# A new program order for a transformer kernel: another choice of scheduler settings per piece

## The chip, the cores and the metric

The kernel runs on one core of a Trainium2 chip. The core has five engines that run their own instruction streams and meet only at semaphores: TensorE (PE) multiplies matrices, VectorE (DVE) and ScalarE (ACT) work element by element, GpSimd (POOL) does so more slowly, and SyncE (SP) starts the transfers between HBM and the on-chip memory. Matmuls write into eight banks of 128x512 numbers of 32 bits (the tensor ps), which VectorE and ScalarE read. The metric is the device time of one execution in microseconds, lower is better.

## What is computed

Two transformer layers on the same weights: x has 2048 rows of 512 numbers, attention has 32 heads of 16, the hidden layer has 1792.

```
for _ in range(2):
    n = layernorm(x);  q, k, v = split(n @ wqkv)
    p = softmax(q @ k.T / 4)              # per head, 2048 x 2048
    x = x + (p @ v) @ wo
    x = x + gelu(layernorm(x) @ w1 + b1) @ w2 + b2
```

Almost all of the element work is the exponential of the scores: 2 layers, 32 heads, 2048 x 2048 numbers each.

## The kernel before

**Cells.** The transposed scores are made in cells of 128 keys by 512 queries (a cell of the last stage joins two heads of 256 queries). There are 4096 of them, each one matmul (score, L1404; the instruction appears at L1413). A pass has up to 64 cells: four heads, each in one group of 32 rows of TensorE's array, by 16 blocks of keys. Cells of different row groups run beside each other; two or three of them make a slot, in as many banks that lie side by side.

**Two ways through the exponential.** ScalarE's exp (exps, instruction at L1853) takes the two or three banks of a slot in one instruction and writes pt. VectorE's way takes one cell at a time: dfirst (L1568, instruction at L1570) turns the score into the bits of a 16-bit power of two in the buffer du; then, for a pair of such cells, dchain (L1673) makes three shifted copies. The first copy is made by GpSimd (L1687) or VectorE, the other two by VectorE in one instruction (L1692), or one each by GpSimd (L1700) and VectorE (L1698). The four copies are multiplied on TensorE by values with four weights (v and vc), so that a VectorE cell needs four value matmuls where a ScalarE cell needs one (pvs, L1869, instructions at L1917; L1925 pads a round of four with zero columns). Where TensorE would stand idle for long, fill matmuls (L1401) keep it running. Some buffers lie over tensors that are not in use at the time, so the same work shows up as du, kt, v, q or g.

**Which cells may go to VectorE.** Blocks of keys 4 to 8 in layer 0 and 1, 4, 7, 10, 13 in layer 1 (KD), so 5 of 16; any of them may also go to ScalarE.

**The rest.** Layer norms (L760 to L786), projections and the hidden layer (matmuls at L653, read out by VectorE), gelu on ScalarE (L1128, with a table load before and after), output projection and residuals run between the cells, as the due times in post allow (a share of the scores of the stage, when). Weights stream through four buffers (wload, on SyncE).

**What sets the order.** No engine chooses at run time. At build time a list scheduler (_Sched.run, L450) plays the whole kernel through with a cost for each instruction (0.065 + 0.4267n us for an exp of n banks, 0.682 for dfirst, 0.15 + 0.45n for a GpSimd shift of n cells, 0.2132 for a round of matmuls), always issues what can start first, by priority among what can start now, and so writes one fixed program per engine, with the waits that the data need. It decides as it goes which cells VectorE takes: attach adds cells to a score group that is about to be issued, as long as banks and buffers are free; swap exchanges the last cell of a group of three for a VectorE cell; solo issues one alone. It also decides which engine makes the shifts.

**Settings.** 29 numbers steer these decisions, named in NAMES. Some examples: SWAP, DMAX, BOTH, SOLO, BACK, SIDE, ALONE, TOL, BACKLOG, OPENING, TAIL and AHEAD say when VectorE may take a cell; PSHIFT, PMORE and DUMORE when GpSimd makes shifts; ROUNDS, PVP, PTURG, DUURG, DULOW, DWIDE, RWIDE and PTLOW when value products run and how many rounds in one go; FPRIO, MID and EVAC rank projections; SLACK, LATE and QUEUE concern the scores' own urgency and the banks. A row of ROWS is one setting of all 29. The scores are cut into 160 pieces of 25.6 cells, and PIECES names the row for each. turn (L1446) loads the next row when take (L1450) has counted enough scores. Row 0 is the plain setting; most others differ from it in one to four numbers.

Of the kernel before, what the change touches and what calls it, by code (L numbers as in the profile page):

```python
# [63 lines left out]
    (0.2, 0.3, 0.7, 0.2, 9, 18, 10, 2, 6, 1, 1, 2, 2, 5, 1.5, 1.4, 0.4, 2, 3.5, 24, 3, 4, 0.4, 1.0, 0, 1, 2, 1, 2,),  # L64
    (0.35, 0.3, 0.7, 0.2, 9, 18, 10, 2, 6, 1, 1, 2, 2, 5, 1.5, 1.4, 0.4, 2, 3.5, 24, 3, 4, 0.4, 1.0, 0, 1, 2, 1, 2,),
    (0.5, 0.2, 0.7, 0.2, 9, 18, 10, 2, 6, 1, 1, 2, 2, 5, 1.5, 1.4, 0.4, 2, 3.5, 24, 3, 4, 0.4, 1.0, 0, 1, 2, 1, 2,),
    (0.5, 0.4, 0.7, 0.2, 9, 18, 10, 2, 6, 1, 1, 2, 2, 5, 1.5, 1.4, 0.4, 2, 3.5, 24, 3, 4, 0.4, 1.0, 0, 1, 2, 1, 2,),
    (0.5, 0.3, 0.7, 0.05, 9, 18, 10, 2, 6, 1, 1, 2, 2, 5, 1.5, 1.4, 0.4, 2, 3.5, 24, 3, 4, 0.4, 1.0, 0, 1, 2, 1, 2,),
    (0.5, 0.3, 0.7, 0.2, 9, 10, 10, 2, 6, 1, 1, 2, 2, 5, 1.5, 1.4, 0.4, 2, 3.5, 24, 3, 4, 0.4, 1.0, 0, 1, 2, 1, 2,),
    (0.5, 0.3, 0.7, 0.2, 9, 14, 10, 2, 6, 1, 1, 2, 2, 5, 1.5, 1.4, 0.4, 2, 3.5, 24, 3, 4, 0.4, 1.0, 0, 1, 2, 1, 2,),  # L70
    (0.5, 0.3, 0.7, 0.2, 9, 18, 6, 2, 6, 1, 1, 2, 2, 5, 1.5, 1.4, 0.4, 2, 3.5, 24, 3, 4, 0.4, 1.0, 0, 1, 2, 1, 2,),
    (0.5, 0.3, 0.7, 0.2, 9, 18, 8, 2, 6, 1, 1, 2, 2, 5, 1.5, 1.4, 0.4, 2, 3.5, 24, 3, 4, 0.4, 1.0, 0, 1, 2, 1, 2,),
    (0.5, 0.3, 0.7, 0.2, 9, 18, 10, 1.2, 6, 1, 1, 2, 2, 5, 1.5, 1.4, 0.4, 2, 3.5, 24, 3, 4, 0.4, 1.0, 0, 1, 2, 1, 2,),
    (0.5, 0.3, 0.7, 0.2, 9, 18, 10, 2, 3, 1, 1, 2, 2, 5, 1.5, 1.4, 0.4, 2, 3.5, 24, 3, 4, 0.4, 1.0, 0, 1, 2, 1, 2,),
    (0.5, 0.3, 0.7, 0.2, 9, 18, 10, 2, 6, 2, 1, 2, 2, 5, 1.5, 1.4, 0.4, 2, 3.5, 24, 3, 4, 0.4, 1.0, 0, 1, 2, 1, 2,),
    (0.5, 0.3, 0.7, 0.2, 9, 18, 10, 2, 6, 3, 1, 2, 2, 5, 1.5, 1.4, 0.4, 2, 3.5, 24, 3, 4, 0.4, 1.0, 0, 1, 2, 1, 2,),
    (0.5, 0.3, 0.7, 0.2, 9, 18, 10, 2, 6, 1, 1, 2, 2, 3, 1.5, 1.4, 0.4, 2, 3.5, 24, 3, 4, 0.4, 1.0, 0, 1, 2, 1, 2,),
# [4 lines left out]
    (0.5, 0.3, 0.7, 0.2, 9, 18, 10, 2, 6, 1, 1, 2, 2, 5, 1.5, 1.4, 0.4, 2, 2.0, 24, 3, 4, 0.4, 1.0, 0, 1, 2, 1, 2,),  # L82
    (0.5, 0.3, 0.7, 0.2, 9, 18, 10, 2, 6, 1, 1, 2, 2, 5, 1.5, 1.4, 0.4, 2, 3.5, 12, 3, 4, 0.4, 1.0, 0, 1, 2, 1, 2,),
    (0.5, 0.3, 0.7, 0.2, 9, 18, 10, 2, 6, 1, 1, 2, 2, 5, 1.5, 1.4, 0.4, 2, 3.5, 24, 3, 4, 0.0, 1.0, 0, 1, 2, 1, 2,),
    (0.5, 0.3, 0.7, 0.2, 9, 18, 10, 2, 6, 1, 1, 2, 2, 5, 1.5, 1.4, 0.4, 2, 3.5, 24, 3, 4, 0.4, 1.5, 0, 1, 2, 1, 2,),
# [4 lines left out]
    (0.5, 0.3, 0.7, 0.2, 9, 18, 10, 2, 6, 1, 1, 2, 2, 5, 1.5, 1.4, 0.4, 2, 3.5, 24, 3, 4, 0.4, 1.0, 0, 1, 2, 1, 1,),  # L90
    (0.5, 0.3, 0.7, 0.2, 9, 18, 10, 2, 6, 1, 1, 2, 2, 5, 1.5, 1.4, 0.4, 2, 3.5, 24, 3, 4, 0.4, 1.0, 0, 1, 2, 1, 5,),
    (0.5, 0.4, 0.7, 0.2, 9, 18, 10, 2, 6, 1, 1, 2, 2, 8, 1.5, 1.4, 0.4, 2, 3.5, 24, 3, 4, 0.4, 1.0, 9, 1, 2, 2, 2,),
    (0.5, 0.3, 0.7, 0.5, 9, 18, 10, 2, 6, 1, 1, 2, 2, 5, 1.5, 1.4, 0.4, 2, 3.5, 24, 3, 4, 0.4, 1.0, 9, 1, 2, 1, 2,),
    (0.5, 0.3, 0.7, 0.05, 9, 18, 10, 2, 6, 3, 1, 2, 2, 5, 1.5, 1.4, 0.4, 2, 3.5, 24, 3, 4, 0.4, 1.0, 0, 1, 2, 1, 2,),
    (0.5, 0.3, 0.7, 0.35, 9, 18, 10, 2, 6, 1, 1, 2, 2, 5, 1.5, 1.7, 0.4, 3, 3.5, 24, 3, 4, 0.4, 1.0, 0, 1, 2, 1, 2,),
    (0.5, 0.3, 0.7, 0.2, 9, 18, 10, 2, 6, 1, 1, 2, 2, 5, 1.5, 1.7, 0.4, 3, 3.5, 24, 3, 4, 0.4, 1.0, 0, 1, 2, 1, 2,),
    (0.5, 0.3, 0.7, 0.2, 9, 18, 10, 2, 6, 1, 1, 2, 2, 5, 1.5, 1.4, 0.4, 2, 3.5, 24, 3, 4, 0.4, 1.0, 0, 2, 2, 1, 1,),
    (0.5, 0.3, 0.7, 0.2, 9, 18, 10, 2, 6, 1, 0, 2, 2, 5, 1.5, 1.4, 0.4, 2, 3.5, 24, 3, 4, 0.4, 0.6, 0, 1, 2, 1, 2,),
    (0.5, 0.3, 0.7, 0.2, 9, 18, 10, 1.2, 6, 1, 1, 2, 2, 5, 1.5, 1.4, 0.4, 2, 3.5, 24, 3, 4, 0.4, 1.0, 0, 2, 2, 1, 2,),
    (0.5, 0.3, 0.8, 0.2, 9, 18, 10, 2, 6, 1, 0, 2, 2, 5, 1.5, 1.4, 0.4, 2, 3.5, 24, 3, 4, 0.4, 1.0, 0, 1, 2, 1, 2,),  # L100
    (0.5, 0.3, 0.7, 0.2, 9, 18, 10, 2, 6, 3, 1, 2, 2, 5, 1.5, 1.4, 0.4, 1, 3.5, 24, 3, 4, 0.0, 1.0, 0, 1, 2, 1, 2,),
    (0.5, 0.3, 0.7, 0.2, 9, 10, 10, 2, 6, 0, 1, 2, 2, 5, 1.5, 1.4, 0.4, 2, 3.5, 24, 3, 4, 0.4, 1.0, 0, 1, 2, 1, 2,),
    (0.5, 0.3, 0.7, 0.2, 9, 18, 10, 2, 6, 1, 1, 2, 2, 5, 2.2, 0.9, 0.4, 2, 3.5, 24, 3, 6, 0.4, 1.0, 0, 1, 2, 1, 2,),
    (0.5, 0.3, 0.55, 0.2, 9, 18, 10, 2, 6, 1, 1, 2, 3, 5, 1.5, 1.4, 0.4, 2, 3.5, 24, 3, 4, 0.4, 1.0, 0, 1, 2, 1, 2,),
    (0.5, 0.3, 0.7, 0.2, 9, 18, 13, 2, 6, 1, 1, 2, 2, 5, 1.5, 0.9, 0.4, 2, 3.5, 24, 3, 4, 0.4, 1.0, 0, 1, 2, 1, 2,),
    (0.5, 0.3, 0.7, 0.2, 9, 18, 10, 2, 6, 1, 1, 2, 2, 8, 1.5, 1.4, 0.4, 1, 3.5, 24, 3, 4, 0.4, 1.0, 0, 1, 2, 1, 2,),
    (0.5, 0.2, 0.7, 0.2, 9, 10, 10, 2, 6, 1, 1, 2, 2, 5, 0.9, 1.4, 9.5, 2, 3.5, 24, 3, 4, 0.4, 1.0, 0, 1, 2, 1, 2,),
    (0.5, 0.3, 0.7, 0.2, 9, 18, 10, 2, 6, 1, 1, 3, 2, 5, 1.5, 1.4, 0.4, 2, 3.5, 24, 3, 4, 0.4, 0.6, 0, 1, 2, 2, 2,),
    (0.5, 0.2, 0.7, 0.2, 9, 18, 10, 2, 6, 1, 1, 2, 2, 5, 1.5, 1.4, 0.4, 2, 3.5, 24, 3, 4, 0.4, 1.0, 1.0, 1, 2, 1, 2,),
    (0.5, 0.3, 0.7, 0.05, 9, 18, 10, 2, 3, 1, 1, 2, 2, 5, 1.5, 1.4, 9.5, 2, 3.5, 24, 3, 4, 0.4, 1.0, 0, 1, 2, 1, 2,),  # L110
    (0.5, 0.3, 0.7, 0.2, 9, 18, 10, 2, 6, 1, 1, 2, 2, 8, 1.5, 1.4, 0.4, 2, 6, 24, 3, 6, 0.4, 1.0, 0, 1, 2, 0.5, 2,),
    (0.5, 0.3, 0.7, 0.2, 9, 18, 10, 2, 6, 1, 1, 2, 2, 5, 1.5, 1.4, 0.4, 1, 3.5, 24, 3, 4, 0.0, 1.0, 0, 1, 2, 1, 2,),
    (0.35, 0.3, 0.8, 0.2, 9, 18, 10, 2, 6, 1, 1, 2, 2, 5, 1.5, 1.4, 0.4, 2, 3.5, 24, 5, 4, 0.4, 1.0, 0, 1, 0, 1, 2,),
    (0.5, 0.3, 0.7, 0.2, 9, 18, 10, 2, 6, 1, 1, 2, 2, 5, 1.5, 1.4, 0.4, 1, 3.5, 32, 3, 4, 0.4, 1.0, 9, 1, 2, 1, 1,),
# [6 lines left out]
    (0.5, 0.3, 0.7, 0.5, 9, 18, 10, 2, 6, 2, 1, 2, 2, 5, 1.5, 1.4, 0.4, 2, 3.5, 24, 3, 4, 0.4, 1.0, 0, 1, 2, 1, 2,),  # L121
    (0.5, 0.3, 0.7, 0.2, 9, 18, 10, 2, 6, 2, 1, 2, 3, 5, 1.5, 1.4, 0.4, 2, 3.5, 24, 3, 4, 0.4, 1.0, 0, 1, 2, 1, 2,),
    (0.5, 0.3, 0.7, 0.35, 9, 18, 10, 2, 6, 1, 1, 2, 2, 5, 1.5, 0.9, 0.4, 3, 3.5, 24, 3, 4, 0.4, 1.0, 0, 1, 2, 1, 3,),
)
PIECES = (10, 10, 15, 18, 18, 43, 56, 38, 30, 38, 38, 28, 8, 0, 60, 60, 48, 21, 43, 35, 46, 0, 1, 45, 45, 49, 4, 11, 41, 25, 57, 24, 20, 31, 15, 1,
          35, 2, 2, 27, 44, 0, 2, 2, 29, 12, 17, 0, 0, 1, 1, 0, 4, 59, 43, 0, 26, 34, 37, 57, 41, 34, 13, 46, 47, 47, 47, 0, 34, 49, 13, 19, 17, 32,
          36, 41, 27, 17, 23, 52, 0, 11, 0, 0, 44, 52, 12, 54, 40, 25, 37, 0, 0, 39, 0, 50, 50, 26, 0, 0, 33, 50, 6, 18, 22, 0, 0, 25, 25, 0, 0, 5,
          42, 16, 53, 0, 36, 12, 0, 55, 34, 18, 53, 3, 0, 46, 0, 0, 58, 0, 0, 0, 46, 25, 25, 41, 44, 13, 12, 12, 17, 20, 12, 12, 7, 54, 25, 28, 0, 0,
          58, 29, 10, 10, 8, 51, 0, 9, 14, 0)
# [513 lines left out]
class _Plan:  # L643
# [802 lines left out]
    def turn(self):  # L1446
        self.piece += 1
        globals().update(zip(NAMES, ROWS[PIECES[self.piece]]))

    def take(self, c):  # L1450
        self.scored += 1
        self.left[c[0]] -= 1
        self.due[c[0]] += 1
        if self.piece + 1 < len(PIECES) and self.scored * len(PIECES) >= (self.piece + 1) * self.total:
            self.turn()
# [573 lines left out]
```

## Time and profile before

| | us |
|---|---|
| median of 3 runs | 1489.41 (1488.92 to 1489.61) |
| the profiled execution | 1490.43 |
| its span, first to last instruction | 1488.6 |
| ScalarE busy | 1457.6 |
| TensorE busy | 1432.6 |
| VectorE busy | 1353.7 |
| GpSimd busy | 942.6 |

Shares are of the span. The busy time of TensorE is to be read with care: its matmuls overlap and their ends are modelled. A group's line in the profile shows the line of code, engine, operation, what is written and read, the count, the busy time, the mean time of one instruction, and the idle time of the engine before it with what ended it.

### The profile page before, as it was taken

To read this page: it belongs to the slowest core of one execution; us is meant where nothing else is said; L and a number is where in the kernel's file an instruction comes from. 1 tells how busy PE (TensorE), PEld (TensorE's weight loads), DVE (VectorE), ACT (ScalarE), POOL (GpSimd) and SP (SyncE) were. 2 spreads that over 40 slices of the span, in tenths; PEclk is the share of its full clock that TensorE was granted. 3 is DMA by queue.
4 is the path that set the end of the run, shared out by engine and by line. 5 is a ranking of instruction groups with operands and counts; after the bars stand their busy time and mean duration, and the time that the engine had idled before them with its cause. 6 is when DMAs were issued, how large, how long until landed. Compare 5 with 4: busy or idle time off the path is not lost.

```text
span 1488.6 us, 46274 instructions
## 1 busy us (share of the span) xinstructions
PE 1432.6 (96%) x20012; PEld 436.7 (29%) x20012; DVE 1353.7 (91%) x2332; ACT 1457.6 (98%) x1387; POOL 942.6 (63%) x1032
## 2 busy tenths in 40 slices
PE   8999999999999999999999999999999999999999
PEld 2222222222222222222222222222222222334345
DVE  6589999999998999989879899999989999999994
ACT  7999999999999999999999999999999999999996
POOL 4347657676665776757556575667667667766751
PEclk9999999999999999999999999999999999999999
DMA  6100001153121430214421431001143104411021
GB/s 171 30 2 2 1 15 31 40 157 91 37 44 58 143 87 27 55 38 132 117 65 44 144 107 37 23 2 37 37 129 100 51 23 129 143 25 44 17 66 38
DMA packets 135798, 94.47 MB, mean 63 GB/s; under 512 B 36525, under 2 KB 134574, under 8 KB 135598
## 3 DMA queue, kind: packets, MB, share of 16 engines
q1 hardware_dynamic: 135598, 91.52, 22.1%
q8 instruction: 160, 2.62, 0.7%
q14 instruction: 40, 0.33, 0.1%
HBM read 79.70 MB, written 4.19 MB: 56 GB/s over the span
## 4 chain that ended last, share of the span: by engine, by line
ACT 49%; PE 37%; DVE 12%; POOL 1%; DMA 1%; issue 1%; SPq 0%
ACT pt L1853 42%; PE ps L653 12%; PE ps L1413 12%; PE ps L1917 12%; DVE du L1570 5%; ACT g L1128 3%; DVE du L1692 2%; DVE kt L1570 1%; ACT kt L1853 1%; ACT q L1853 1%; ACT L1128 1%; PE ps L1401 1%; DVE x L1167 1%; ACT L1853 1%; DVE g L1107 0%
## 5 line engine op out<-in xcount | busy, mean ns | idle before, releaser
L1853 ACT ACTIVATE pt<-ps 128x1024 bf16<-128x1024 f32 (+1 forms) x1253 | 1306.9, 1177 | 8.0 <-PE ps L1413 6.1
L1570 DVE TENSOR_SCALAR du<-ps 128x512 uint16<-128x512 f32 x853 | 564.9, 680 | 40.3 <-PE ps L1413 35.8
L1687 POOL TENSOR_SCALAR du<-du 128x1024 uint16<-128x1024 uint16 (+1 forms) x429 | 445.8, 1044 | 232.4 <-DVE du L1570 97.4
L1413 PE MATMUL ps<-qp,kt 32*128 32x512 bf16 x4096 | 548.4, 384 | 25.2 <-ACT pt L1853 13.6
L1917 PE MATMUL ps<-pt,v 128*17 128x512 bf16 (+1 forms) x3159 | 388.2, 359 | 3.4 <-ACT pt L1853 1.1
L1917 PE MATMUL ps<-du,vc 128*17 128x512 bf16 (+1 forms) x2874 | 346.9, 357 | 3.6 <-POOL v L1700 0.8
L1413 PEld LDWEIGHTS ps<-qp,kt 32*128 32x128 bf16 x4096 | 139.5, 91 | 576.5 <-ACT pt L1853 200.5
L1692 DVE TENSOR_SCALAR du<-du 128x2048 uint16<-128x2048 uint16 x336 | 245.4, 744 | 4.2 <-POOL du L1687 4.2
L1917 PE MATMUL ps<-du,v 128*17 128x512 bf16 (+1 forms) x958 | 158.6, 359 | 4.9 <-DVE xt L932 1.6
L1925 PE MATMUL ps<-b2row,zero 128*17 128x512 bf16 x788 | 145.5, 381 | 0.0
L653 PE MATMUL ps<-xf,wr 128*32 128x512 bf16 (+1 forms) x1888 | 128.5, 364 | 1.4 <-DVE g L1107 1.1
L1917 PEld LDWEIGHTS ps<-pt,v 128*17 128x17 bf16 x3159 | 95.6, 88 | 103.8 <-issue 70.4
L1361 POOL TENSOR_SCALAR qp<-q,mask 128x512 bf16<-128x512 bf16 (+1 forms) x91 | 61.4, 675 | 94.3 <-PE ps L1413 42.0
L1570 DVE TENSOR_SCALAR kt<-ps 128x512 uint16<-128x512 f32 x165 | 109.9, 681 | 10.5 <-PE ps L1413 9.7
L1917 PEld LDWEIGHTS ps<-du,vc 128*17 128x17 bf16 x2874 | 96.3, 89 | 76.2 <-issue 42.8
L1687 POOL TENSOR_SCALAR kt<-kt 128x1024 uint16<-128x1024 uint16 x83 | 86.9, 1048 | 49.3 <-DVE du L1692 23.1
L653 PE MATMUL ps<-wr,g 128*32 128x512 bf16 x1408 | 105.0, 383 | 1.1 <-DMA wr<-in_B_w_dram 0.5
L1342 POOL TENSOR_SCALAR vc<-v 128x680 bf16<-128x680 bf16 (+2 forms) x126 | 87.4, 693 | 25.4 <-DVE du L1692 8.2
L1700 POOL TENSOR_SCALAR du<-du 128x1024 uint16<-128x1024 uint16 (+1 forms) x93 | 97.1, 1044 | 8.4 <-DVE du L1692 4.4
L1917 PE MATMUL ps<-kt,vc 128*17 128x512 bf16 (+1 forms) x615 | 96.0, 339 | 1.2 <-DVE kt L1692 0.8
L1107 DVE TENSOR_SCALAR g<-ps,hb1t 128x512 bf16<-128x512 f32 (+1 forms) x112 | 79.0, 706 | 3.9 <-PE ps L653 3.6
L786 POOL TENSOR_SCALAR xln<-x,rstd,nmr 128x512 bf16<-128x512 bf16 x58 | 47.0, 818 | 21.9 <-DVE du L1692 10.9
(110 smaller groups left out, 1451.8 us busy)
## 6 DMA issues: line engine op xcount, KB each, us to landing
wr<-in_B_w_dram SPq DMA_DIRECT2D x228, 256.0 KB, 2.9
wr<-in_A_wqkv_dram SPq DMA_DIRECT2D x24, 256.0 KB, 2.9
x<-in_A_x_dram SPq DMA_DIRECT2D x7, 512.0 KB, 4.1
wr<-in_A_wo_dram SPq DMA_DIRECT2D x10, 256.0 KB, 3.3
kept<-x SPq DMA_DIRECT2D x4, 512.0 KB, 3.5
x<-kept SPq DMA_DIRECT2D x4, 512.0 KB, 3.9
out_dram<-x SPq DMA_DIRECT2D x16, 128.0 KB, 2.2
g<-in_A_wqkv_dram SPq DMA_DIRECT2D x3, 512.0 KB, 5.5
```

The costliest lines, as they stand in the source:

```text
L653: return [lambda e, a=a: e.matmul(out[32 * a:32 * a + 32, :], lhsT=lhsT[:, 32 * a:32 * a + 32], rhs=rhs, start=start, stop=stop, tile_posi ...
L1107: yield _Op("dve", 0.21 + n / 966, lambda e, fc=fc, pb=pb: e.tensor_scalar(T["G"][:, fc, q], pb, T["HB1T"][:, fc:fc + 1], None, op0=ALU.ad ...
L1342: yield _Op("pool", 0.15 + 0.133 * len(js), lambda e, i=i, w=w, v=v, js=js, src=src: e.tensor_scalar(T["VC"][:, v % 2, i, js[0]:js[-1] + 1 ...
L1361: yield _Op("pool", 0.27 + 0.42 * w / 512, lambda e, s=s, q=q, i=i, t=t, w=w: e.tensor_scalar(T["QP"][:, s, w * i:w * i + w], q, T["MASK"] ...
L1413: return (lambda e: e.matmul(o, lhsT=lhsT, rhs=rhs, start=True, stop=True, tile_position=(32 * a, 0)), ["K%d.%d.%d" % (l, gb, kt // 4), "Q ...
L1570: yield _Op("dve", 0.682, lambda e: e.tensor_scalar(u, self.bank(b), E_SCALE, E_BIAS, op0=ALU.mult, op1=ALU.add), reads=["B.%d" % b], writ ...
L1687: one = _Op("pool", 0.15 + 0.45 * n, lambda e, a=a, b=b: e.tensor_scalar(b, a, float(SHIFT), 1.0, op0=ALU.add, op1=ALU.mult), reads=key[0] ...
L1692: two = _Op("dve", 0.152 + 0.266 * n, lambda e: e.tensor_scalar(U[:, 2:4, 0:n, :], U[:, 0:2, 0:n, :], 2 * SHIFT, None, op0=ALU.add), reads ...
L1700: more = _Op("pool", 0.15 + 0.45 * n, lambda e, a=a, c=c: e.tensor_scalar(c, a, float(2 * SHIFT), 1.0, op0=ALU.add, op1=ALU.mult), reads=k ...
L1853: yield _Op("act", 0.065 + 0.4267 * n, lambda e, src=src, dst=dst: e.activation(out=dst, in_=src, func=ACT.Exp, scale=0.25), reads=["B.%d" ...
L1917: op.fns.append(lambda e, o=o, lhsT=q[0][0][m], rhs=q[0][1][:, n * m:n * m + n], a=a, st=st, sp=sp: e.matmul(o, lhsT=lhsT, rhs=rhs, start= ...
L1925: op.fns.append(lambda e, o=self.bank(b)[32 * a:32 * a + 17, :], rhs=rhs, a=a, st=not begun[a], sp=end: e.matmul(o, lhsT=T["ZERO"][:, 0:17 ...
```

## The change

The code of the scheduler and its costs stay, as does the work: the same cells, tiles, buffers and semaphores. Three things differ.

- ROWS has 55 rows instead of 61. Row 0 and 41 others are in both tables; 19 are gone and 13 are new.
- PIECES names another row for nearly every piece. Only 8 of the 160 pieces have the settings that they had. 38 pieces have row 0, against 32. The new list was picked with five partial orders kept at each step, the old one with one.
- take turns to the next piece at the whole part of (piece + 1) x 4096 / 160 scores, where it was the first count at or above it.

```
 ROWS = (
     (0.5, 0.3, 0.7, 0.2, 9, 18, 10, 2, 6, 1, 1, 2, 2, 5, 1.5, 1.4, 0.4, 2, 3.5, 24, 3, 4, 0.4, 1.0, 0, 1, 2, 1, 2,),
-    (0.2, 0.3, 0.7, 0.2, 9, 18, 10, 2, 6, 1, 1, 2, 2, 5, 1.5, 1.4, 0.4, 2, 3.5, 24, 3, 4, 0.4, 1.0, 0, 1, 2, 1, 2,),
...
+    (0.5, 0.3, 0.7, 0.5, 9, 18, 10, 2, 6, 1, 1, 2, 2, 5, 1.5, 1.4, 0.4, 2, 3.5, 24, 3, 4, 0.4, 1.0, 0, 1, 2, 1, 2,),
...
-PIECES = (10, 10, 15, 18, 18, 43, 56, 38, 30, 38, 38, 28, 8, 0, 60, 60, 48, 21, 43, 35, 46, 0, 1, 45, 45, 49, 4, 11, 41, 25, 57, 24, 20, 31, 15, 1,
...
+PIECES = (0, 0, 33, 17, 33, 44, 42, 38, 0, 9, 53, 0, 10, 25, 0, 3, 0, 0, 10, 2, 35, 27, 27, 44, 11, 31, 31, 35, 0, 13, 29, 51, 43, 0, 20, 48, 48, 0,
...
-        if self.piece + 1 < len(PIECES) and self.scored * len(PIECES) >= (self.piece + 1) * self.total:
+        if self.piece + 1 < len(PIECES) and self.scored >= (self.piece + 1) * self.total // len(PIECES):
             self.turn()
```

How the settings are spread over the pieces, before and after, counted as pieces with at least one of the named settings off row 0: who takes a cell 69 and 60, who makes the shifts 32 and 29, value products 65 and 71, projections and scores 38 and 35. Single settings that change much: ROUNDS=1 in 13 and 18 pieces, ROUNDS=3 in 8 and 6, BOTH=2 in 6 and 1, SOLO=0 in 6 and 10, SWAP off 0.5 in 12 and 7, TOL off 0.2 in 11 and 17.

## The prediction

> **What bounds the kernel now.** I read the span and the engines' shares first, then the chain and the costliest groups, then what ScalarE waited for, and last a table by stage, for all instructions and for the first VectorE step of a score cell alone. (A cell is one 128x512 block of scores; there are 4096.)
>
> ```profile
> span 1488.6 us, 46274 instructions
> PE 1432.6 (96%) x20012; PEld 436.7 (29%) x20012; DVE 1353.7 (91%) x2332; ACT 1457.6 (98%) x1387; POOL 942.6 (63%) x1032
> ...
> ACT 49%; PE 37%; DVE 12%; POOL 1%; DMA 1%; issue 1%; SPq 0%
> ...
> L1853 ACT ACTIVATE pt<-ps 128x1024 bf16<-128x1024 f32 (+1 forms) x1253 | 1306.9, 1177 | 8.0 <-PE ps L1413 6.1
> L1570 DVE TENSOR_SCALAR du<-ps 128x512 uint16<-128x512 f32 x853 | 564.9, 680 | 40.3 <-PE ps L1413 35.8
> L1687 POOL TENSOR_SCALAR du<-du 128x1024 uint16<-128x1024 uint16 (+1 forms) x429 | 445.8, 1044 | 232.4 <-DVE du L1570 97.4
> ...
> L1692 DVE TENSOR_SCALAR du<-du 128x2048 uint16<-128x2048 uint16 x336 | 245.4, 744 | 4.2 <-POOL du L1687 4.2
> ```
>
> ScalarE (ACT) is busy 98% and stands idle 31 us in all. Its waits from 98 to 1440 us, and the same stretch cut into stages (PE, PEld, DVE, ACT, POOL busy, then clock and DMA):
>
> ```profile
> ACT pt L1853 <- PE ps L1413: 5.5, 23, 0.5
> ```
>
> ```profile
> 98.00:480.00 382.00, 368.60 (x4783) 102.17 (x4775) 360.01 (x609) 381.04 (x352) 254.38 (x272) 1.00 0.17 44
> 480.00:720.00 240.00, 233.32 (x3077) 65.03 (x3069) 227.14 (x390) 237.47 (x234) 164.72 (x170) 1.00 0.31 88
> 720.00:780.00 60.00, 56.27 (x748) 16.40 (x740) 45.00 (x79) 59.26 (x52) 30.60 (x36) 1.00 0.26 72
> 780.00:1100.00 320.00, 306.10 (x4028) 86.26 (x4024) 303.77 (x513) 318.46 (x298) 204.49 (x234) 1.00 0.20 57
> 1100.00:1440.00 340.00, 331.00 (x5188) 112.73 (x5180) 325.69 (x558) 337.89 (x327) 234.82 (x252) 1.00 0.24 68
> ```
>
> In these 1342 us ScalarE is idle 7.9 us, VectorE (DVE) 80.4, TensorE (PE) 46.7. So a better order can hardly win by removing waits of ScalarE: what is left to win is ScalarE's work itself, by giving cells to VectorE and GpSimd (POOL). The count of cells that VectorE takes in 40 us varies though each stage does the same work:
>
> ```profile
> 120.00:160.00 40.00, 24.24 (x38) 1.00 0.01 2
> ...
> 440.00:480.00 40.00, 17.28 (x26) 1.00 0.12 35
> ...
> 720.00:760.00 40.00, 8.60 (x13) 1.00 0.25 71
> ...
> 1000.00:1040.00 40.00, 18.24 (x28) 1.00 0.15 30
> ```
>
> Over the 32 such windows from 120 to 1440 us, without the one at the layer change, the mean is 32.6 cells and the standard deviation 3.0.
>
> **The prices.** VectorE took 853 + 165 + 78 = 1096 cells (the groups of its first step into the buffers du, kt and v), so ScalarE took 3000. One cell less on ScalarE: 1306.9 us over the 2835 cells of its largest group is 0.461; a three-bank exp less a two-bank one is 1499 - 1062 = 437 ns. I take 0.45. One cell more on VectorE: 0.68 for the first step, and the shifts, which by the single durations are 314 us (L1692) and 65 us (L1698) over some 550 pairs, so 0.34 a cell: 1.02 together. GpSimd pays 0.52 a cell (1044 ns a pair), against 462 us idle from 98 us on. PE multiplies four values instead of one: three more of the four matmuls that make a round, and a round follows the last by 0.22 us, so 0.16 a cell.
>
> **The change, part by part.** *The table of rows* (61 to 55) issues nothing. *The piece boundary* in take rounds down instead of up: 4096/160 is 25.6 scores a piece, and 128 of the 159 boundaries come one score earlier. At most one decision is taken under another row, between -0.45 and +0.45 us each if it moved a cell; nearest to it are the pieces where two neighbours carry the same row, for which it is nothing, and I take zero. The edit of substance is *PIECES*: only 8 of 160 pieces keep their settings, so nearly all of the program is in another order from the first pieces on. By what the settings touch, pieces with a value off row 0, before to after:
> - who takes a cell (SWAP, DMAX, BOTH, SOLO, BACK, SIDE, ALONE, TOL, BACKLOG, OPENING, TAIL, AHEAD): 69 to 60. This is the term that pays: x cells give -0.45x. From below, as many cells lost as one standard deviation of the sum over 32 windows: 3.0 x 5.7 = 17 cells, +7.6 us. From above, all idle VectorE time outside the layer change, 80.4 - 15.0 = 65.4 us, filled at 1.02: 64 cells, -28.8 us.
> - who does the shifts (PSHIFT, PMORE, DUMORE): 32 to 29. A pair whose second shift goes to GpSimd takes 420 ns (median of L1698) instead of 684 (median of L1692) on VectorE, and 1.05 more on GpSimd. With 123 such pairs now, ten more or fewer are 2.6 us of VectorE, 2.6 cells, 1.2 us either way. Zero taken.
> - which value products run when (ROUNDS, PVP, PTURG, DUURG, DULOW, DWIDE, RWIDE, PTLOW): 65 to 71. Cover: PE has 46.7 us idle and spends 145.5 us on zero columns that pad a round (788 matmuls). With that cover gone, 12 more cells would lay 1.9 us on PE. Zero taken.
> - projections and score slack (FPRIO, MID, EVAC, SLACK, LATE, QUEUE): 38 to 35. They move PE and VectorE work inside a stage, and behind it the weight loads on SyncE's queue and GpSimd's mask, shift and LN instructions. The 228 weight loads land 2.9 us after issue and PE waited 0.5 us for them; DMA engines are 22% busy. If a load came late, one landing, 2.9 us, would be the price. ScalarE's gelus and table loads stay: 7.55 us in each of seven stages.
>
> What stays whatever the order: the first 60 us, in which VectorE takes no cell and ScalarE loses 8.2; the hole after 738 us, where keys and values of layer 1 are still to be projected and no cell may go to VectorE (156 scores in 60 us where 2.86 a microsecond is the rule); and the 27 us after the last exp.
>
> The first term decides. I take 12 cells more: 0.4 per window, an eighth of the scatter between windows with the same work, and 12.2 of 65.4 us of free VectorE time. Why more and not fewer: the settings choose among orders by the durations written in the code, and these are what the trace shows (an exp of n banks 0.065 + 0.4267n, so 1.03 for the mean 2.26 banks, against 1.043; 0.682 against 0.680 for VectorE's step; 0.15 + 0.45n = 1.05 against 1.044 for GpSimd's shift). An order short by these is short on the chip, unless a thing that they lack decides. Sum: -12 x 0.45 = -5.4 us. The profiled execution took 1490.4 us, 1.8 more than its span and 1.0 over the median; 1490.4 - 5.4 = 1485.0 there, and 1489.4 - 5.4 = **1484 us** as a median.
>
> **A rule against the trace.** PE's 96% looks as near to the bound as ScalarE's 98%; against that stand its zero columns and its idle 46.7 us, which pay for 290 moved cells, so no PE term is in the sum. The Trainium skill ("Perfetto Trace Analysis", Identifying the Most-Contended Engine) also says that matmul busy time does not measure how near TensorE is to its limit; by the busy figure alone, 56 us would be the most to win.
>
> **The rivals.**
> 1. *The same split in another order*: VectorE takes 1096 cells give or take 6, gains in one stage given back in the next. For it speaks that a third of the forecast's 0.4 cell in each window would be lost in a scatter of 3.0; against it that 65.4 us of VectorE time are free to be used. Time 1489.4, within 3 us.
> 2. *More is recovered*: a third of the 65.4 us, 21 cells or more. For it speaks that 40 us windows with 36 to 38 cells stand beside some with 26 to 28; against it that VectorE is at 94% in all stages. With a quarter of the 7.9 us of ScalarE idle time, 1489.4 - 21 x 0.45 - 2 = 1478.
> 3. *Slower: VectorE and GpSimd block each other more often.* The shifts of L1692 have a median of 684 ns but reach 1668; 61 of 422 full ones and 30 of 123 at L1698 run over 150 ns longer than the median, 36.8 us together, mostly by starting while a GpSimd shift of 1.05 us runs. The order decides who meets whom. If half as much again is lost, 18.4 us of VectorE, then 18 cells go back to ScalarE: +8.1, 1497.5. It decides from about 19 us lost: 12 us eat up the gain, 7 more cost 3 us. Against it: the scheduler holds a shift back while the other engine's runs. The Trainium skill ("SBUF — State Buffer", Who interferes with whom) states it as a lock on a shared port pair that the first to start keeps for its whole instruction; the longest shift, 684 + 984 ns, agrees with that. By this rule alone every meeting costs up to a whole GpSimd instruction.
>
> **How the numbers follow.** About 0.2% (3 us) is what can be told from no change. Forecast, 1480.4 to 1486.4: 0.42. Rival 2, under 1480.4: 0.18. Rival 1: 0.20. Rival 3, over 1492.4: 0.20. So faster 0.60, same 0.20, slower 0.20. The range reaches to 1475 below (29 to 32 cells) and to 1496 above (15 cells lost), with about 0.06 and 0.12 left out; the forecast's own range is 1480 to 1487.
>
> **What would show it.** VectorE's first step over 1096 by about 12 (right), equal (rival 1) or fewer (wrong); exps of ScalarE correspondingly fewer cells, its busy time near 1452; its waits in the middle still under 10 us; shifts longer than the median still near 37 us in sum (rival 3: 55). The hole at 738 us and the last 27 us unchanged. Wrong would be the whole reading if the time moved by more than 0.45 us for each cell moved: then waits of ScalarE, not its work, had changed.

## The result, and the profile after

The changed kernel takes 1485.93 us in the median of 12 runs (1485.69 to 1488.62), against 1489.6 us before in the same comparison. The ratio is 0.9973, 95% interval 0.9964 to 0.9982: faster by 0.27%, or 3.7 to 4.0 us. The profiled execution took 1485.86 us with a span of 1483.9.

The page of the changed kernel, in the lines that answer to those shown of before (all of its lines of code stand six lower from the tables on: L1853 is L1847 now, L1570 is L1564, L1692 is L1686):

```profile
span 1483.9 us, 46274 instructions
PE 1432.3 (97%) x19973; PEld 433.1 (29%) x19973; DVE 1359.9 (92%) x2351; ACT 1452.2 (98%) x1390; POOL 965.5 (65%) x1049
...
PE 47%; ACT 30%; DVE 22%; POOL 1%; issue 1%; DMA 0%
...
L1847 ACT ACTIVATE pt<-ps 128x1024 bf16<-128x1024 f32 (+1 forms) x1220 | 1264.7, 1174 | 7.6 <-PE ps L1407 5.7
...
L1564 DVE TENSOR_SCALAR du<-ps 128x512 uint16<-128x512 f32 x864 | 570.2, 680 | 35.6 <-PE ps L1407 31.5
...
L1686 DVE TENSOR_SCALAR du<-du 128x2048 uint16<-128x2048 uint16 x323 | 234.2, 741 | 5.0 <-POOL du L1681 4.9
```

ScalarE is busy 5.4 us less (1457.6 to 1452.2) and idle 0.7 us more (31.0 to 31.7): together the 4.7 us by which the span is shorter. VectorE is busy 6.2 us more and GpSimd 22.9 us more; TensorE is as busy as before (1432.6 and 1432.3). VectorE's first step runs 864 + 165 + 80 = 1109 times, by its groups into du, kt and v, 13 more than before; ScalarE does 2987 cells in 1329 exps, where it did 3000 in 1326. The chain that ended last runs through other engines than before: TensorE 47% and VectorE 22%, where ScalarE had 49%. The experiments below show why that matters.

The table by stage, of VectorE's first step alone (busy time, count, granted clock, DMA). The first stage is the one that changed most. Its line of before:

```profile
98.00:480.00 382.00, 199.95 (x305) 1.00 0.17 44
```

The changed kernel:

```profile
98.00:480.00 382.00, 212.16 (x323) 1.00 0.16 44
480.00:720.00 240.00, 128.65 (x197) 1.00 0.31 90
720.00:780.00 60.00, 16.92 (x26) 1.00 0.25 68
780.00:1100.00 320.00, 166.57 (x254) 1.00 0.22 63
1100.00:1440.00 340.00, 184.32 (x280) 1.00 0.23 66
```

Before, the counts were 305, 197, 26, 253 and 281. So 18 cells are won between 98 and 480 us, none in the stages after it, and a few are lost at either end. In that stage VectorE is busy 370.0 us instead of 360.0, and ScalarE's idle time rises from 1.0 to 4.0 us; from 480 to 1440 us ScalarE's idle time falls from 6.9 to 5.2 us. The first stage now, with all engines (PE, PEld, DVE, ACT, POOL):

```profile
98.00:480.00 382.00, 368.72 (x4763) 100.36 (x4755) 370.03 (x633) 378.01 (x359) 268.93 (x281) 1.00 0.16 44
```

The score that opens piece 56 of 160 starts at 520.8 instead of 523.8 us, that of piece 156 at 1420.0 instead of 1424.4: about two thirds of the gain are made in the first third. The layer change at 720 us still has 26 cells in 60 us. From the last exp to the end it takes 26.5 us in both kernels (1462.1 to 1488.6; 1457.4 to 1483.9).

### The profile page after: what moved, and what is told of

Read it like the earlier page. It is cut to its first block, busy times and chain, and to the rows that moved or that the text cites. A ratio compares the mean times of both kernels' runs of the same rounds, so it can differ in the third digit from the quotient of the medians.

```text
span 1483.9 us, 46274 instructions
## 1 busy us (share of the span) xinstructions
PE 1432.3 (97%) x19973; PEld 433.1 (29%) x19973; DVE 1359.9 (92%) x2351; ACT 1452.2 (98%) x1390; POOL 965.5 (65%) x1049
## 4 chain that ended last, share of the span: by engine, by line
PE 47%; ACT 30%; DVE 22%; POOL 1%; issue 1%; DMA 0%
ACT pt L1847 24%; PE ps L1911 16%; PE ps L1407 16%; PE ps L647 15%; DVE du L1564 8%; DVE du L1686 4%; ACT g L1122 3%; DVE kt L1564 1%; DVE stats L754 1%; DVE kt L1686 1%; DVE v L1564 1%; DVE du L1692 1%; ACT L1122 1%; ACT L1847 1%; DVE xt L926 1%
## 5 line engine op out<-in xcount | busy, mean ns | idle before, releaser
L1847 ACT ACTIVATE pt<-ps 128x1024 bf16<-128x1024 f32 (+1 forms) x1220 | 1264.7, 1174 | 7.6 <-PE ps L1407 5.7
L1681 POOL TENSOR_SCALAR du<-du 128x1024 uint16<-128x1024 uint16 (+1 forms) x434 | 452.0, 1046 | 239.8 <-DVE du L1686 96.2
L1564 DVE TENSOR_SCALAR du<-ps 128x512 uint16<-128x512 f32 x864 | 570.2, 680 | 35.6 <-PE ps L1407 31.5
L1911 PE MATMUL ps<-pt,v 128*17 128x512 bf16 (+1 forms) x3069 | 399.2, 359 | 3.7 <-ACT pt L1847 2.2
L1911 PE MATMUL ps<-du,vc 128*17 128x512 bf16 (+1 forms) x2907 | 360.1, 357 | 4.3 <-DVE du L1686 2.2
L1686 DVE TENSOR_SCALAR du<-du 128x2048 uint16<-128x2048 uint16 x323 | 234.2, 741 | 5.0 <-POOL du L1681 4.9
L1911 PE MATMUL ps<-du,v 128*17 128x512 bf16 (+1 forms) x969 | 165.4, 359 | 7.6 <-DVE xt L926 2.2
L1919 PE MATMUL ps<-b2row,zero 128*17 128x512 bf16 x741 | 152.0, 381 | 0.0
L1694 POOL TENSOR_SCALAR du<-du 128x1024 uint16<-128x1024 uint16 (+1 forms) x111 | 115.2, 1038 | 9.9 <-DVE du L1686 3.8
L1564 DVE TENSOR_SCALAR kt<-ps 128x512 uint16<-128x512 f32 x165 | 111.1, 682 | 9.5 <-PE ps L1407 8.4
L1911 PE MATMUL ps<-kt,vc 128*17 128x512 bf16 (+1 forms) x612 | 99.3, 340 | 0.5 <-DVE kt L1692 0.5
```

What stands on the lines that cost most here:

```text
L1564: yield _Op("dve", 0.682, lambda e: e.tensor_scalar(u, self.bank(b), E_SCALE, E_BIAS, op0=ALU.mult, op1=ALU.add), reads=["B.%d" % b], writ ...
L1681: one = _Op("pool", 0.15 + 0.45 * n, lambda e, a=a, b=b: e.tensor_scalar(b, a, float(SHIFT), 1.0, op0=ALU.add, op1=ALU.mult), reads=key[0] ...
L1686: two = _Op("dve", 0.152 + 0.266 * n, lambda e: e.tensor_scalar(U[:, 2:4, 0:n, :], U[:, 0:2, 0:n, :], 2 * SHIFT, None, op0=ALU.add), reads ...
L1694: more = _Op("pool", 0.15 + 0.45 * n, lambda e, a=a, c=c: e.tensor_scalar(c, a, float(2 * SHIFT), 1.0, op0=ALU.add, op1=ALU.mult), reads=k ...
L1847: yield _Op("act", 0.065 + 0.4267 * n, lambda e, src=src, dst=dst: e.activation(out=dst, in_=src, func=ACT.Exp, scale=0.25), reads=["B.%d" ...
L1911: op.fns.append(lambda e, o=o, lhsT=q[0][0][m], rhs=q[0][1][:, n * m:n * m + n], a=a, st=st, sp=sp: e.matmul(o, lhsT=lhsT, rhs=rhs, start= ...
```

## The experiments

All are variants of the changed kernel, each timed beside the kernel before. Two theories were left open by the prediction. *Theory W*: the time is ScalarE's work, and a cell that moves to VectorE saves its price. *Theory O*: a list of settings fits one order only, and out of step with it the engines also wait.

### The parts of the change one by one

Row 0 in every piece:

```diff
-PIECES = (0, 0, 33, 17, 33, 44, 42, 38, 0, 9, 53, 0, 10, 25, 0, 3, 0, 0, 10, 2, ...
+PIECES = (0, 0, 0, 0, 0, 0, 0, 0, 0, 0, 0, 0, 0, 0, 0, 0, 0, 0, 0, 0, ...
```

> The changed kernel with row 0 in all 160 pieces, so no picking at all. The program that comes out has 1077 VectorE cells (before 1096, after 1109). Theory W (the time is ScalarE's work, 0.45 us for a cell): 32 cells fewer than after give +14.4 us, 1500 us, and ScalarE still waits under 10 us in the middle. Theory O (a list of settings also keeps ScalarE from waiting, so an order without it costs more than its cells): the scheduler's own end moves by +17.2 us against after, 1503 us; the 3 us over W would be waits of ScalarE.

Only the boundary put back:

```diff
-        if self.piece + 1 < len(PIECES) and self.scored >= (self.piece + 1) * self.total // len(PIECES):
+        if self.piece + 1 < len(PIECES) and self.scored * len(PIECES) >= (self.piece + 1) * self.total:
```

> The changed kernel with only the piece boundary put back (rounded up). My prediction took zero for this edit, at most 0.45 us for a boundary. The program has 1077 VectorE cells, as many as with row 0 everywhere. Theory W: +14.4 us against after, 1500 us, the same as the plain rows. Theory O: the list is out of step with the state that it was picked for from the first moved boundary on, the scheduler's own end moves by +33.0 us, 1519 us, and the 19 us over W stand in the trace as ScalarE waiting for score matmuls.

The list of before, with the new boundary (ROWS and PIECES of before in the changed kernel):

> The list of before (its rows and pieces) with the new boundary (rounded down): the other part of the change alone. The program has 1064 VectorE cells. Theory W: 45 fewer than after, +20.2 us, 1506 us. Theory O: +30.5 us by the scheduler's own end, 1516 us, with 10 us of ScalarE waits.

The new list in pieces 0 to 79, the old one in 80 to 159:

> The new list for pieces 0 to 79, the old one for pieces 80 to 159, new boundary. The program has 1097 VectorE cells, 12 fewer than after, one more than before. Theory W: +5.4 us against after, 1491 us. Theory O: +12.2 us by the scheduler's own end, 1498 us: rows that were good in the old order are not good behind another first half, so the second half costs as much as unpicked rows. If the old second half kept its worth wherever it stands, the first half's gain alone (738.0 to 734.6 us at piece 80) would remain: 1486 us.

Measured, with the accounts of each profile (ScalarE's idle time is the span less its busy time; cells are VectorE's). Each ratio is to runs of the kernel before in the same comparison, 1489.2 us for the four variants:

| kernel | cells | median us | ratio to before, 95% | span | ScalarE busy | ScalarE idle |
|---|---|---|---|---|---|---|
| before | 1096 | 1489.6 | 1 | 1488.6 | 1457.6 | 31.0 |
| after | 1109 | 1485.9 | 0.9973 (0.9964 to 0.9982) | 1483.9 | 1452.2 | 31.7 |
| row 0 everywhere | 1077 | 1500.3 | 1.0073 (1.0058 to 1.0088) | 1497.6 | 1464.8 | 32.8 |
| boundary back | 1077 | 1516.6 | 1.0183 (1.0168 to 1.0198) | 1515.0 | 1466.4 | 48.6 |
| old list, new boundary | 1064 | 1510.4 | 1.0142 (1.0125 to 1.0159) | 1508.7 | 1470.1 | 38.6 |
| half new, half old | 1097 | 1499.4 | 1.0067 (1.0052 to 1.0082) | 1495.6 | 1457.9 | 37.7 |

The second and third kernels, in which one part of the change is undone, are slower than before by 1.8% and 1.4%, and slower than with no picking at all. Neither part of the change works alone. A boundary that comes one score later puts another score group under a row, and from there on the program is another one: the list's rows then do worse than row 0. Both theories have a part in it. ScalarE's busy time goes with the cells, at 0.39 to 0.47 us each (12.6 us for the 32 cells of row 0, 17.9 for 45, 5.7 for 12). For row 0 everywhere that is all: theory W gave 1500 us and theory O 1503, measured are 1500.3, and ScalarE's idle time is 32.8 us against 31.7. An order out of step makes ScalarE wait on top of that. In the kernel with the boundary put back, these are its longest waits from 98 us on (who waited for whom, total, times, longest):

```profile
ACT pt L1847 <- PE ps L1407: 12.8, 25, 1.4
ACT pt L1847 <- PE ps L1911: 8.1, 3, 3.9
ACT v L1847 <- PE ps L1407: 1.9, 4, 1.1
```

In the changed kernel the longest of these lines is

```profile
ACT pt L1847 <- PE ps L1407: 5.7, 16, 0.6
```

Row 0 everywhere and the boundary put back have equally many cells, and 16 us lie between them: ScalarE's idle time accounts for 15.8 of the 17.4 us between their spans. Theory W fails for the three lists out of step (1500, 1506 and 1491 us), and theory O is right to 6 us (1519 expected, 1516.6 measured; 1516 and 1510.4; 1498 and 1499.4). The fourth kernel shows that the old second half was worth little behind the new first half: at 1499.4 it is hardly better than row 0 from the start.

### Work taken from one engine, in the same order

The kernels of this part keep every instruction of the changed kernel in its place. One bank less in 51 exps:

```diff
-            src = self.bank(self.slots[sl][0], n).rearrange("p (j q) -> p j q", j=n)
-            dst = self.unit(run)
+            self.ring = getattr(self, "ring", 0) + (u >= 200 and n > 1 and run[0] < PT_RING)
+            m = n - (u >= 200 and n > 1 and run[0] < PT_RING and self.ring % 20 == 0)
+            src = self.bank(self.slots[sl][0], m).rearrange("p (j q) -> p j q", j=m)
+            dst = self.unit(run)[:, 0:m, :]
...
```

> The changed kernel, every instruction in the same order, but 51 exps of ScalarE (spread evenly over the exps from the 200th on that write the ring pt) read and write one bank fewer than they should, so these 51 cells are left out of the exponential. That is 51 x 0.437 = 22.3 us less work on ScalarE and nothing else. If ScalarE's work sets the time (theory W): 1486 - 22 = 1464 us. If TensorE and VectorE are as tight in this fixed order (the chain of after has TensorE at 47%, ScalarE at 30%, VectorE at 22%): less than half of it comes off, 1475 us or more.

It took 1485.24 us, 0.7 us less than the changed kernel. This is the result that I had least expected. By the price of a bank the cut is 22.3 us; in the trace ScalarE's busy time falls by 14.9 us, and its idle time rises by 13.5. Page, and its longest wait:

```profile
span 1482.5 us, 46274 instructions
PE 1431.4 (97%) x19973; PEld 432.4 (29%) x19973; DVE 1359.9 (92%) x2351; ACT 1437.3 (97%) x1390; POOL 965.6 (65%) x1049
...
PE 54%; DVE 27%; ACT 18%; POOL 1%; issue 1%; DMA 0%; SPq 0%
```

```profile
ACT pt L1850 <- PE ps L1407: 16.5, 52, 0.6
```

ScalarE, 98% busy and with hardly a wait, was not what held the time: TensorE is busy as long, and a ScalarE that is done sooner waits for the next scores: its waits for score matmuls in exps that write pt rise from 5.7 to 16.5 us. Next, more work on VectorE:

```diff
+        self.nfirst = getattr(self, "nfirst", 0) + 1
+        more, extra, far = self.nfirst > 200 and self.nfirst % 30 == 0, [], []
+        if more:
+            x = self.T["DU"][pair["du"]][:, 3, j, :]
+            extra, far = [lambda e: e.tensor_scalar(x, self.bank(b), ...)], ["DU.%d.3.%d" % (pair["du"], j)]
-        yield _Op("dve", 0.682, lambda e: e.tensor_scalar(u, self.bank(b), ...),
+        yield _Op("dve", 0.682, extra + [lambda e: e.tensor_scalar(u, self.bank(b), ...)],
...
```

> The changed kernel in the same order, but 30 of the 1109 first steps on VectorE (every 30th from the 200th on) are done twice, the first time into a part of the buffer that is written again later. 30 x 0.68 = 20 us more work on VectorE alone. VectorE is idle 74 us after the first 98 us. If that idle time can take it (theory W): within 3 us of 1486. If VectorE is as tight as ScalarE: +10 to +20 us, 1496 to 1506.

It took 1497.11 us, 11.2 more, for 30 instructions of 0.68 us, 20.3 us in sum. VectorE's busy time rose by 15.0. So 74 us of idle time took in between a quarter (of the 15.0) and 45% (of the 20.3) of it: the gaps of VectorE are mostly not where the added work is. Then less work on TensorE:

```diff
+                    full = n == 512 and len(got) == 4 and all(begun) and not end and self.scored > 400
+                    self.nround = getattr(self, "nround", 0) + full
+                    c = 256 if full and self.nround % 6 == 0 else n
...
-                            o = self.bank(b)[32 * a:32 * a + 17, n * m:n * m + n]
+                            o = self.bank(b)[32 * a:32 * a + 17, n * m:n * m + c]
...
```

> The changed kernel in the same order, with every sixth full round of value matmuls (198 of 1188, four matmuls each) 256 columns wide instead of 512; half of these products is left out. By the pitch of a round, 0.22 us, that is 198 x 0.107 = 21 us less work on TensorE and nothing else. Theory T (TensorE's stream alone sets the time, as ScalarE's does not): 1486 - 21 = 1465 us. Theory B (the three engines are balanced, each holds the time up when another gets faster): under 7 us off, 1479 us or more. If TensorE's granted clock falls as in e8_fill, the gain is smaller for that reason; then the clock shows it.

The same cut together with the one in the exps:

> The cuts of e9_peless and of e5_actless together: 21 us less on TensorE, 22 us less on ScalarE, VectorE as it was. Theory T: 1465 us, no more than e9_peless. Theory B: more than the two single gains together, about 8 to 12 us off, 1474 to 1478 us; VectorE is then the wall that is left.

Both of them, and a cut in VectorE's first steps (of its lines, the one that sets the width):

```diff
...
+        w = 256 if self.nfirst > 200 and pair["du"] < self.own and self.nfirst % 9 == 0 else 512
...
```

> As e10_peact, and 74 of VectorE's first steps read and write 256 columns instead of 512: 74 x 0.2 = 15 us less on VectorE (0.48 us for 256 columns at L1101 against 0.68). Theory B: now all three have 15 to 22 us less to do, and the time falls by 15 us or more, to 1471 us or less. Theory T: 1465 us as in e9_peless and e10_peact. Had the waits between the engines, and not their work, set the time, it would stay above 1478.

| taken away, same order | busy time that went (TensorE, ScalarE, VectorE) | median us | less than after |
|---|---|---|---|
| ScalarE | 0.9, 14.9, 0 | 1485.2 | 0.7 |
| TensorE | 12.3, 2.8, -0.5 | 1482.8 | 3.2 |
| TensorE and ScalarE | 13.4, 17.4, 0.2 | 1480.0 | 5.9 |
| all three | 13.6, 17.6, 12.0 | 1479.2 | 6.8 |

Theory T, TensorE alone, is out: it gives 3.2 us for 12.3. Theory B is right in kind for the first two kernels (under 7 us expected, 3.2 measured; 8 to 12 and 5.9) and fails for the third: with 12 to 18 us less on each of the three engines the time falls by 6.8 us, not by 15. At 1479.2 us that is the case which the last expectation put above 1478: the waits between the engines, and not their work alone, set the time. TensorE and ScalarE together gain more than the sum of the two single gains (5.9 against 3.9), so each does hold the other up. But in a fixed order more than half of what is taken away is lost again. A likely reason is that an instruction comes no sooner than the latest of those that it waits for, and that the cuts were spread evenly and not put where the chain runs; this was not shown, and what the rest waits for was not followed further.

### The meetings of VectorE and GpSimd

```diff
         if op.eng == "pe" and op.mode != self.mode:
             t -= SW
-        if op.eng == "pool":
-            at, op.lock = max(t, self.clock["pool"]), None
...
-        if op.port and op.eng == "dve":
...
         return t
```

> The changed kernel with the part of the scheduler left out that holds VectorE's shifts back while a GpSimd instruction runs and the other way round. The order is another one; the program has 1143 VectorE cells, 34 more than after. Theory W by cells alone, at 0.40 us (the price between e1_plain and after): -13.6 us, 1472 us. My rival 3 (both engines block each other): shifts that run over 150 ns longer than the median go from 36 us in sum to 70 us or more, VectorE falls behind its order, others wait for it, and the time is 1490 us or more.

1601.37 us: 115 us more, with 34 cells more on VectorE, where theory W gave 1472 us. The groups of the shifts, GpSimd's first, then VectorE's three copies as one pair and as one:

```profile
L1668 POOL TENSOR_SCALAR du<-du 128x1024 uint16<-128x1024 uint16 (+1 forms) x447 | 515.8, 1157 | 267.9 <-DVE du L1551 255.0
...
L1673 DVE TENSOR_SCALAR du<-du 128x2048 uint16<-128x2048 uint16 (+1 forms) x309 | 263.6, 860 | 9.8 <-POOL du L1668 9.6
...
L1679 DVE TENSOR_SCALAR du<-du 128x1024 uint16<-128x1024 uint16 (+1 forms) x138 | 112.0, 814 | 3.8 <-POOL du L1668 3.8
```

The mean of VectorE's two-copy shift (du) goes from 741 to 860 ns. Counted one by one, 273 of its 568 shifts run over 150 ns longer than the median of after and lose 142.7 us (after: 84 of 552, 35.6 us); GpSimd's lose 81 us, where it was 3.2. ScalarE stands idle 109 us between 98 us and its last exp. So the loss on VectorE is 107 us more, and the time 115 us more. Not all of the 115 us is that loss: with 34 cells more VectorE has some 35 us more to do by the price of 1.02 us a cell, and the granted clock is 0.989 to 0.994 in the four runs. How the 115 us divide was not tried. The Trainium skill ("SBUF — State Buffer", Who interferes with whom) says of VectorE's two-port modes that whichever of the two engines starts first keeps the shared ports for its whole instruction and the other blocks. That both engines' shifts are longer here agrees with it; the mode of a shift is not in the trace.

### The fill matmuls

```diff
-            w, o = lhs[:, m * a:m * a + m], self.bank(b)[m * a:m * a + m, :]
+            w, o = lhs[:, m * a:m * a + m], self.bank(b)[m * a:m * a + m, 0:64]
...
-            fns.append(lambda e, o=o, w=w, a=a, m=m: e.matmul(o, lhsT=w, rhs=rhs,
+            fns.append(lambda e, o=o, w=w, a=a, m=m: e.matmul(o, lhsT=w, rhs=rhs[:, 0:64],
```

> The changed kernel in the same order with the fill matmuls of TensorE (L1395, those into idle time) 64 columns wide instead of 512. They feed nothing. My prediction let PE's idle time and its zero work be cover that costs nothing: then within 3 us of 1486. If they are needed to keep TensorE's clock or the matmuls behind them start slower without them: slower than 1489 us, with longer score matmuls or a granted clock under 1.00.

1498.44 us, 12.5 more, although TensorE is busy 11 us less. The granted clock of the profiled run is 0.983 instead of 1.000. Over the six runs the time goes with it: 1494.1 us at 0.990, 1497.7 to 1499.1 at 0.985 to 0.987, 1500.8 and 1500.9 at 0.983. By that slope, about 1 us for each 0.001, the clock alone is enough for the 12.5 us (an estimate from these runs). It does not fall evenly. TensorE's busy time around the layer change, in windows of 4 us (busy, clock, DMA):

```profile
720.00:724.00 4.00, 3.52 (x46) 1.00 0.02 5
724.00:728.00 4.00, 3.27 (x50) 1.00 0.02 4
728.00:732.00 4.00, 3.07 (x46) 1.00 0.17 34
732.00:736.00 4.00, 3.48 (x52) 0.69 0.49 165
736.00:740.00 4.00, 4.00 (x38) 0.50 0.44 135
```

In the 12 us from 720 us TensorE is busy 77 to 88%, and then the clock is at half for 6.8 us, from 733.6 us on. The last 3.4 us before the drop:

```profile
730.20:733.60 3.40, 2.24 (x38) 0.99 0.40 80
```

In the changed kernel the clock is 1.00 from 720 to 740 us.

### Another pick

A new list for all 160 pieces in the changed kernel, with a table of rows of its own (not shown), picked from 110 rows with eight orders kept; 159 pieces have other settings than after:

```diff
-PIECES = (0, 0, 33, 17, 33, 44, 42, 38, 0, 9, 53, 0, 10, 25, ...
+PIECES = (1, 2, 3, 4, 5, 6, 7, 8, 9, 10, 11, 12, 0, 13, ...
```

> The changed kernel with another list, picked anew for all 160 pieces: 110 rows to choose from, eight partial orders kept at each step, each row judged by how far the scheduler has come four plain pieces later (scores issued, value products and side work left over). One piece of 160 has the same settings as after. The program has 1112 VectorE cells, 3 more than after. By cells at 0.41 us: 1.2 us less than after, 1484.7 us. By the scheduler's own end, which the other orders kept to within a few us: 1.0 us less, 1485 us. Both say that a list picked with more care from more rows lands where the changed kernel is. If the pick after had been a lucky one on the chip, an independent pick would fall back toward the kernel before, 1489 us; if the chip has something that both lists miss, it could differ by more than 3 us either way.

1490.97 us (1487.44 to 1493.78 in 11 runs), ratio to before 1.0009 (1.0000 to 1.0018): 5 us over the changed kernel, with 3 more cells on VectorE and by the scheduler's own end 1 us shorter. So it did fall back to the kernel before, as expected for the case that the pick of after had been a lucky one on the chip. The page of its profiled run, which took 1488.11:

```profile
span 1486.3 us, 46051 instructions
PE 1427.3 (96%) x19852; PEld 434.4 (29%) x19852; DVE 1373.2 (92%) x2355; ACT 1452.5 (98%) x1385; POOL 986.0 (66%) x1069
```

ScalarE's busy time is that of after (1452.5 against 1452.2), its idle time 2.1 us more. Two things that the scheduler does not count, or not fully, differ. First, VectorE's shifts meet GpSimd more often: 113 of 554 run long and lose 50.9 us, against 35.6. Second, TensorE has less to do and stands idle 51.5 us between 98 us and the last exp, against 43.3, and in 8 of the 11 runs its granted clock is not 1.000 throughout: in the three runs at 1.000 the time is 1487.4 to 1488.1, at 0.997 to 0.999 it is 1489.7 to 1491.6, at 0.995 it is 1493.8. About 2 us are there at full clock, and some 3 more go with the lower clock. What costs the 2 us, the meetings or something else, was not tried by itself.

## Why the prediction was right, and where its reason was not

**The number.** 1484 us was forecast, 1485.9 measured, inside the forecast's own range of 1480 to 1487 (1480.4 to 1486.4 where the chances are given). The cells moved (12; 13 measured) and ScalarE's busy time (about 1452; 1452.2) were right. The 12 was a choice within wide bounds (17 cells lost to 64 won), an eighth of a scatter, so that it came true within one cell is in part luck. The price per cell was a little high: 5.4 us for 13 cells is 0.41, not 0.45, since three more exps were needed for fewer cells. ScalarE's idle time, taken as unchanged, rose by 0.7. And the profiled execution of before had run 1.0 us above its median, that of after at its median, so that 4.7 us of span are 3.7 us of median.

**Where the cells came from.** I spread them evenly, 0.4 a window. They came from the first 480 us alone, where VectorE is now busy 370.0 of 382 us instead of 360.0. From there to 1440 us the new order has no more cells than the old one; what it still wins, some 1.5 us, goes with 1.7 us less of ScalarE's idle time.

**The boundary** was put down at zero. Within the change it has no price of its own, since the new list was picked with it. Undone by itself it costs 31 us, the largest mis-sizing in the working. The reason I gave, that at most one decision per boundary falls under another row, counted the decision and not what follows from it: all later decisions start from another state.

**What stays** stayed: the first 60 us without VectorE cells, the layer change, the last 27 us, and the gelus.

**Cover on TensorE.** I took its 46.7 us of idle time and its zero columns as cover and put no TensorE term in the sum. Yet 12.3 us less busy time on TensorE in the same order gained 3.2 us, more than 14.9 us less on ScalarE, so TensorE holds the time up as well. The fills, which the sum did not name, are not free either: cut to an eighth they cost 12.5 us by the clock. No run left out the zero columns themselves.

**Rival 3** did not come (the shifts that run long lost 36.8 us before and 35.6 after), and the scheduler's care has a part in that: without it the loss is 142.7 us. The mechanism is real, and the price was probably too low: I let 18 us lost on VectorE cost 8.1 us, 0.45 per us, but VectorE's 15.0 us of added busy time cost 11.2. The 115 us for 107 us lost point the same way, with other things mixed in.

**Why the sign could be told.** I argued that an order which is short by the scheduler's durations is short on the chip, unless a thing that they lack decides. For the four variants with other lists or boundaries it held: 17.2, 33.0, 30.5 and 12.2 us longer than after by the scheduler's own end, 14.4, 30.7, 24.5 and 13.5 us measured. It did not hold for the other pick, which was 1 us shorter by those durations and 5 us longer on the chip, with two such things in its trace. A forecast of 5 us by this argument is near its limit, and that the change kept its gain where the other pick lost it is luck as far as the argument goes. The trace of before could not show it, and my 0.20 each for no change and for slower stood for that.

**The reading itself.** "What is left to win is ScalarE's work itself" was right as an account and wrong as a cause. 14.9 us less busy time on ScalarE in the same order gained 0.7 us. That the time still goes with ScalarE's work from one order of the scheduler to the next may come from each order being built to keep all engines close to full; no run shows this by itself. What the pages show is that a new order also packs TensorE's work anew: its matmuls are 39 fewer (20012 to 19973), with 13 more cells of four products each, as fewer zero columns pad the rounds (741 instead of 788) and fewer fills run (752 instead of 780). I had named the sign by which the reading would fall, more than 0.45 us per cell; after against before stays under it (3.7 us for 13 cells), but the boundary put back gives 31 us for 32 cells. There the waits had changed.

## What to carry to other kernels

In a kernel with three engines over 90% busy, a stage without waits on the busiest engine does not show that this engine's work sets the time; take some of its work away in the same order and see. A list of choices that a greedy scheduler was tuned with belongs to exactly one state of it: here an edit of one step in its counting undid all of the tuning, and more. So such a list is picked again after every change, and a few us of it are only known on the chip. Fills and hold-backs that look like waste are worth a test before they count as cover.

## What was not expected of the hardware

With the narrow fills the granted TensorE clock fell to 0.50 seven times before the last exp, for 3.4, 6.8 or 17.1 us. In the 3.4 us before these drops TensorE was still busy 37 to 69% by the trace, and in the 12 us before them it never stood idle for over 2.2 us in one piece (0.6 us before the drop at 733.6 us). The Trainium skill ("TensorE: Matmul & The Clock Gate", What's actually happening) describes a clock that goes to half after an idle window of about 3.4 us; here no such window preceded any of the drops.

How many matmuls TensorE starts tells more than how long it is busy. I cut the traces into the steps of 3.41 us in which their clock records change, and counted a matmul of 512 columns as one, a narrower one by its share. The seven drops came behind steps with 15.5 to 22.5 matmuls. In all fourteen traces, from 20 us to the last exp, no step at full clock with more than 26 had a drop behind it, and none with fewer than 22 kept the clock; between 22 and 26 both occur. The lowest step has 30 matmuls in the kernel before and 27 in the changed kernel. The other pick comes down to 22, and the same program ran at 0.995 to 1.000 from run to run, with its time going over 6 us. Whether the one comes from the other is open: the kernel with one bank less in 51 exps comes down to 23 and ran at 1.000 each time.

When VectorE and GpSimd meet, both lose: without the scheduler's care GpSimd's own shift (du) took 1157 ns in the mean instead of 1046.
